# Attention scores in four quarters of TensorE, keys kept in halves of a tile, and a later landing in the planner's model

## The chip, the cores and the metric

One core of a Trainium2 chip runs the kernel. The metric is the device time of one execution in microseconds; of several runs the median counts. The trace that is read here comes from one profiled execution of the kernel before the change.

## What is computed

Three layers follow each other on 4 sequences of 576 tokens with 512 features (2304 tokens, 18 tiles of 128 tokens). The reference, cut to what matters:

```python
scores = scale * q @ k.T                     # 8 heads of 64, per sequence
mask = (rel >= 0) & (rel < 128)              # each query sees itself and 127 keys before it
attn = softmax(where(mask, scores - slope * |rel|, -1e9))
x = attn @ v                                 # attention
u = x + (relu(x.T @ w_tok1) @ w_tok2).T      # token mixing, 256 hidden
x = u + relu(u @ w_ch1) @ w_ch2              # first wide layer, 1536 hidden
out = x + relu(layernorm(x) * g @ w2_ch1) @ w2_ch2   # second wide layer, 2048 hidden
```

## The kernel before

**Attention.** A loop goes over the 18 tiles of 128 queries. `packed` issues the scores of one tile and the values of the tile two before it as one block on TensorE (PE). Heads are taken in two halves c of four heads. For each head pair p and each head j of the pair, one matmul contracts the 64 features on 64 rows of the array (row half j), against the keys of the tile before and of the own tile: 64 rows, 128 queries as columns, 256 keys streamed. The program has 8 such matmuls for a tile; the profile shows each fp32 matmul as two instructions. `softmax` then folds the two key tiles into one: a predicated copy (L631) on VectorE (DVE) puts the earlier key's score where the own key lies after the query, so that each query keeps 128 scores. Bias, minimum, Exp on ScalarE (ACT), four transposes on PE, a copy and two masks on GpSimd (POOL) follow. Keys lie in a ring of four tiles (`keys`); tile i uses slot i % 4, and where that is slot 0 the matmul reads slots 0 and 3.

**Token mixing** runs in between: tok1 and tok2 matmuls (L440 to L442, L735 to L737) of one sequence after the other. They need `wt1` (5 pieces) and `wt2` (4 pieces).

**Conversions.** All weights come as 64-bit floats. `load_f64` fetches two strided views of a piece (`rh`, one buffer; `rw`, two buffers), ACT makes `e` from `rh` (L416), and DVE makes the fp32 weight in four instructions (L419 to L431). The next load of `rh` waits until `e` has been made. Attention contains 21 conversions: 9 of `wt1` and `wt2`, then 12 of the first wide layer. Of these 12, six go straight into the six buffers `w`, and six are written to DRAM (`stage_w`) and fetched again later. The first wide layer's first eight tiles need 24 such pieces in six steps: two pieces of w_ch1 and two of w_ch2 for a step. Each step is a group of "products" (matmuls b, L993 to L995), and its "second" (matmuls acc, L1048 to L1050) runs one step later. The order in which the pieces are used: products 0, products 1, second 0, products 2, second 1, products 3, second 2, and so on, two pieces each.

**The planner.** The order of all instructions on every engine is made when the kernel is built. `Plan.order` simulates the operations with fixed costs and latencies; each engine takes the ready operation with the lowest rank. The chip then runs each engine's list strictly in that order; only data is waited for, the planned times are not. What a conversion looks like in that model:

```python
LAT = {"PE": 400, "DVE": 260, "ACT": 290, "POOL": 180, "DMA": 4000, "CTL": 0}
ready[j] = max(ready[j], free[e] + self.lat(e, ...))      # an operation that needs k's result
rh = buf("raw", [P, DM, 4], I16, "rh", 1)                 # one buffer
op({"DMA": max(P * n * 8 / 360, 500)}, emit, writes=[x])  # load of rh, of rw
op({"ACT": act(n)}, ..., [rh], [e])                       # act(n) = 170 + 0.9 n
```

So in the model the next load of `rh` starts no sooner than load cost + 4000 + act(n) + 290 ns after the one before it. A piece has n = 256 (`wt1`), 288 (`wt2`) or 512 columns.

Of the kernel before, what the change touches and what calls it, by code (L numbers as in the profile page):

```python
# [10 lines left out]
F32 = mybir.dt.float32  # L11
# [3 lines left out]
I32 = mybir.dt.int32  # L15
# [8 lines left out]
B, H, S, D = 4, 8, 576, 64  # L24
P = 128
DM = H * D
NT = B * S
NTILE = NT // P
# [4 lines left out]
RING = 4  # L33
# [9 lines left out]
X_SHIFT, STAGE_SHIFT = -20, -20  # L43

STAGE_RATES = {(0, 2): 2, (1, 0): 2}
WARM, WARM_NS = 10, 320
WT_SHIFT, WT_START, WT_STEP, SHIFT_AT, W_START, W_STEP = 0, 2, 1, 7, 12, 2
SIGN16, EXP16 = 0x80008000 - (1 << 32), 0x7F807F80
# [2 lines left out]
def batches_of(i):  # L51

    out, t, end = [], i * P, (i + 1) * P
    while t < end:
        b, s = divmod(t, S)
        n = min(end - t, S - s)
        out.append((b, t - i * P, n, s))
        t += n
    return out
# [43 lines left out]
class Plan:  # L103
# [11 lines left out]
    HOLD_ANY = False  # L115
    AHEAD = 2000
    SPARE = {"DVE": 1200, "ACT": 0}
    LAT = {"PE": 400, "DVE": 260, "ACT": 290, "POOL": 180, "DMA": 4000, "CTL": 0}

    def __init__(self):  # L120
        self.pools, self.ops, self.rings, self.ctl = {}, [], {}, {}
# [4 lines left out]
    def buf(self, pool, shape, dtype, tag, bufs=1):  # L126
        b = Buf(self, pool, shape, dtype, tag, bufs)
        ring = self.rings.setdefault((pool, tag), [])
        if len(ring) >= bufs:
            b.after = [ring[-bufs]]  # L130
        if ring:
            b.behind = ring[-1]
        ring.append(b)
        return b
# [176 lines left out]
def pe(n):  # L311
    return 2.6 + n / 2.4


def block_kernel(tc, qT, kT, v, wt1, wt2, wa1, wa2, wb1, wb2, g, bias, out):
    nc = tc.nc
    NF1, NF2 = FF1 // P, FF2 // P
    pl = Plan()
    buf = pl.buf

    def op(cost, emit, reads=(), writes=(), behind=()):
        return pl.op(cost, (lambda e: emit()) if len(cost) == 1 else emit, reads, writes, behind)
# [26 lines left out]
    after = buf("const", [P, P], F32, "after")  # L349
# [31 lines left out]
    def load_f64(src, k, n, dst=None, get=None):  # L381

        rh = buf("raw", [P, DM, 4], I16, "rh", 1)
        rw = buf("raw", [P, DM, 2], U32, "rw", 2)
        e = buf("cvt", [P, DM], BF16, "e", 1)
        s = buf("cvt", [P, DM], BF16, "s", 1)  # L390
        m = buf("cvt", [P, DM], U32, "m", 1)
        at = k * P * n * 8
        flat = src.bitcast(U8).rearrange("r b -> (r b)")

        def rows(x, first):
            return x.rearrange("p n t -> p (n t)"), flat[first:first + P * n * 8].rearrange("(p b) -> p b", p=P)

        def head(dt):
            return rh.t[:, :n, 3].bitcast(dt) if dt != I16 else rh.t[:, :n, 3]

        def load_half(x, first):
            def emit():
                out, in_ = rows(x.t[:, :n].bitcast(U8), first)
                nc.sync.dma_start(out=out, in_=in_)

            op({"DMA": max(P * n * 8 / 360, 500)}, emit, writes=[x])

        load_half(rh, at)
        load_half(rw, at + 3)

        def half(x):
            return x.t[:, :n].bitcast(I32)

        op({"ACT": act(n)}, lambda: nc.scalar.activation(  # L416
            out=e.t[:, :n], in_=head(BF16), func=AF.Copy, scale=2.0 ** -116), [rh], [e])

        op({"DVE": 1.3 * dve(n // 2, True)}, lambda: nc.vector.tensor_scalar(  # L419
            half(s), half(e), 3, EXP16, ALU.logical_shift_left, ALU.bitwise_and), [e], [s])  # L420
        op({"DVE": 1.3 * dve(n // 2)}, lambda: nc.vector.scalar_tensor_tensor(
            out=half(s), in0=half(e), scalar=SIGN16, in1=half(s), op0=ALU.bitwise_and, op1=ALU.bitwise_or), [e], [s])
        op({"DVE": 1.3 * dve(n, True)}, lambda: nc.vector.tensor_scalar(
            m.t[:, :n], rw.t[:, :n, 0], 4, None, ALU.logical_shift_left), [rw], [m])
        if dst is None:
            dst = y = buf("cvt", [P, DM], F32, "y", 2)

            def get():
                return y.t[:, :n]

        op({"DVE": 1.3 * dve(n)}, lambda: nc.vector.scalar_tensor_tensor(  # L431
            out=get(), in0=m.t[:, :n], scalar=2.0 ** 32, in1=s.t[:, :n], op0=ALU.add, op1=ALU.mult), [m, s], [dst])
        return dst, get
# [28 lines left out]
    src = {"a1": wa1, "a2": wa2, "b1": wb1, "b2": wb2}  # L462
    wtiles, staged = [], {}
    used = [0]

    def convert_w(x, dst=None, get=None):

# [53 lines left out]
        return [buf("hid", [P, 2, S + P], F32R, "few" + p) for p in "hl"]  # L521


    keys = buf("att", [P, RING, H // 2, P], F32, "keys")
    wt1h, wt1l = ([buf("tok", [P, 5, TOK], F32R, f"wt1{x}{odd}") for odd in range(2)] for x in "hl")
    wt2h, wt2l = few()
    vs, qs = {}, {}
# [1 line left out]
    def load_qk(i):  # L529
        r = i % RING  # L530
        b = qs[i] = buf("att", [P, H // 2, P], F32, "q", Q_BUFS)
        op({"DMA": 1000}, lambda: nc.sync.dma_start(out=keys.t[:, r].rearrange("p h t -> p (h t)"), in_=kT[i]),
           writes=[(keys, r)])
        load(b, lambda: b.t.rearrange("p h t -> p (h t)"), P * DM * 4, qT[i])

    def load_v(i):
# [25 lines left out]

    def keys_of(i):

        s = i % RING
        if starts_batch(i):
            return [i], 0, 0, (s, s + 1, 1)
        table = 3 if len(batches_of(i)) > 1 else 2 if len(batches_of(i - 1)) > 1 else 1
        if s == 0:
            return [i, i - 1], 0, table, (0, RING, RING - 1)  # L570
        return [i - 1, i], 1, table, (s - 1, s + 1, 1)

    pv = buf("psb", [P, H // 2, P], F32, "ps_v")
    rs_t, xh_t, xl_t = {}, {}, {}
# [1 line left out]
    ps_t, pf_t = {}, {}  # L576

    def packed(i, i2):

        parts, ready = [], []
        if i is not None:
            tiles, own, table, (a0, a1, a2) = keys_of(i)
            w = len(tiles) * P
            x = qs[i]
            for c in range(2):
                ps_t[i, c] = buf("psa", [P, 2, 2, 2 * P], F32, "ps_s", 2)  # L590

                def scores(c=c, ps=ps_t[i, c]):
                    for p in range(2):
                        for j in range(2):
                            r = slice(j * D, (j + 1) * D)
                            nc.tensor.matmul(ps.t[:, j, p, :w], x.t[r, 2 * c + p], keys.t[r, a0:a1:a2, 2 * c + p],  # L596
                                             start=True, stop=True)

                parts.append((4 * pe(2 * w), scores, [x] + [(keys, t % RING) for t in tiles], [ps_t[i, c]]))
        if i2 is not None:  # L600
            tiles2 = keys_of(i2)[0]
            na = len(tiles2)
            for c in range(2):
                def values(c=c, pf=pf_t[i2, c]):
                    for p in range(2):
                        for a, kt in enumerate((i2, i2 - 1)[:na]):
                            for j in range(2):
                                nc.tensor.matmul(pv.t[j * D:(j + 1) * D, 2 * c + p], vs[kt].t[:, 4 * c + 2 * p + j],  # L608
                                                 pf.t[:, a, 2 * p + j], start=(a == 0), stop=(a == na - 1))

                parts.append((na * 440, values, [(pf_t[i2, c], a) for a in range(na)] + [vs[kt] for kt in tiles2],
                              [(pv, c)]))

        before = None
        for k, (cost, emit, reads, writes) in enumerate(parts):
            also = parts[k + 1:] if k == 0 else []
            now = op({"PE": cost + (200 if k in (0, len(parts) - 1) else 0)}, emit,
               reads + [x for p in also for x in p[2]], writes + [x for p in also for x in p[3]])
            if before is not None:
                pl.chain[before] = now  # L620
            before = now

    def softmax(i, c):

        tiles, own, table, _ = keys_of(i)
        na = len(tiles)
        ps = ps_t[i, c]
        o = slice(own * P, (own + 1) * P)
        if na == 2:
            b = slice((1 - own) * P, (2 - own) * P)  # L630
            op({"DVE": 690}, lambda: nc.vector.copy_predicated(  # L631
                ps.t[:, :, :, o], after.t.bitcast(I32).unsqueeze(1).unsqueeze(1).to_broadcast([P, 2, 2, P]),
                ps.t[:, :, :, b]), [ps, after], [ps])
        t = buf("att", [P, 4, P], F32, "t", T_BUFS)
        mn = buf("small", [P, 4], F32, "mn", 3)
        for m in range(4):
            op({"DVE": 358}, lambda m=m: nc.vector.tensor_tensor_reduce(  # L637
                out=t.t[:, m], in0=ps.t[:, m % 2, m // 2, o], in1=bias_sb.t[:, table, 4 * c + m],
# [6 lines left out]
        for m in range(4):  # L645
            op({"ACT": 580}, lambda m=m: nc.scalar.activation(  # L646
                out=pr.t[:, m], in_=t.t[:, m], func=AF.Exp, bias=mn.t[:, m:m + 1], scale=-1.0,
# [433 lines left out]
    def swap(close=(), open_=()):  # L1081
# [6 lines left out]

        pl.control(emit, close, [n for n, _ in open_])

    rest = attention()

# [25 lines left out]
    for s in range(len(steps) + 1):  # L1120
# [5 lines left out]
        layer, c, tiles, n = steps[s]  # L1126
        hid = {}
        if len(tiles) == 2:
            parts, ns = two_blocks(w1, xs, hid), (4, 4)
        else:  # L1130
            parts, ns = seven_products(w1, xs, keep, s == len(steps) - 1, hid), (2, 3, 3, 0)
# [81 lines left out]
```

## Time and profile before

| | us |
|---|---|
| median of 3 runs | 855.08 (854.54 to 855.89) |
| profiled execution, its own time | 856.19 |
| its span in the trace | 854.5 |

The 1.7 us between the span and the execution's own time lie around the program. Engines are PE (matmul), PEld (weight load), DVE, ACT, POOL and SP (the queue that issues most DMAs). A matmul's end is modelled in the trace, so busy PE may hide small gaps; starts are measured.

### The profile page before, as it was taken

To read this page: it belongs to the slowest core of one execution; us is meant where nothing else is said; L and a number is where in the kernel's file an instruction comes from. 1 tells how busy PE (TensorE), PEld (TensorE's weight loads), DVE (VectorE), ACT (ScalarE), POOL (GpSimd) and SP (SyncE) were. 2 spreads that over 40 slices of the span, in tenths; PEclk is the share of its full clock that TensorE was granted. 3 is DMA by queue.
4 is the path that set the end of the run, shared out by engine and by line. 5 is a ranking of instruction groups with operands and counts; after the bars stand their busy time and mean duration, and the time that the engine had idled before them with its cause. 6 is when DMAs were issued, how large, how long until landed. Compare 5 with 4: busy or idle time off the path is not lost.

```text
span 854.5 us, 13205 instructions
## 1 busy us (share of the span) xinstructions
PE 830.8 (97%) x4478; PEld 685.8 (80%) x4478; DVE 638.1 (75%) x1311; ACT 394.3 (46%) x952; POOL 338.5 (40%) x353
## 2 busy tenths in 40 slices
PE   7999999979999999999999999999999999999997
PEld 6777888758888887788887888788889888888885
DVE  5787777987887989987888956988676855555554
ACT  6888766643434535334357323336357422222220
POOL 2685445554433556532235524614234612221110
PEclk9999999999999999999999999999999999999999
DMA  8678736457677699978762521887477762221112
GB/s 296 187 207 265 242 103 213 146 179 241 200 234 240 228 324 337 348 252 268 264 210 74 178 92 48 264 263 258 154 259 234 247 198 74 74 75 49 50 50 98
DMA packets 73698, 164.96 MB, mean 193 GB/s; under 512 B 8352, under 2 KB 8480, under 8 KB 73632
## 3 DMA queue, kind: packets, MB, share of 16 engines
q1 hardware_dynamic: 73152, 162.83, 57.5%
q0 software_dynamic: 480, 1.31, 0.7%
q8 instruction: 35, 0.57, 0.3%
q14 instruction: 31, 0.25, 0.1%
HBM read 131.34 MB, written 31.46 MB: 191 GB/s over the span
## 4 chain that ended last, share of the span: by engine, by line
PE 83%; DVE 7%; ACT 4%; DMA 2%; issue 2%; POOL 1%; SPq 1%; ACTq 0%; DVEq 0%; POOLq 0%
PE acc L1048 12%; PE acc L1050 12%; PE acc L1049 12%; PE b L993 9%; PE b L995 9%; PE b L994 9%; PE ps_v L608 3%; PE ps_s L596 3%; PE p L848 1%; PE b L442 1%; PE b L441 1%; PE b L440 1%; PE ps_t L653 1%; DVE st L374 1%; PE tok L735 1%
## 5 line engine op out<-in xcount | busy, mean ns | idle before, releaser
L1053 DVE TENSOR_TENSOR u<-acc,u 128x512 f32<-128x512 f32 x252 | 172.9, 687 | 64.0 <-PE acc L1050 60.6
L1048 PE MATMUL acc<-w2h,hh 128*128 128x512 f32 x504 | 198.6, 394 | 5.3 <-DVE u L1053 4.7
L1050 PE MATMUL acc<-w2h,hl 128*128 128x512 f32 x504 | 196.6, 390 | 0.3 <-DVE hl L926 0.2
L1049 PE MATMUL acc<-w2l,hh 128*128 128x512 f32 x504 | 196.5, 390 | 0.0
L924 ACT ACTIVATE hh<-b 128x512 fp32r<-128x512 f32 (+1 forms) x140 | 74.5, 552 | 262.8 <-PE b L995 226.4
L993 PE MATMUL b<-xh,w1h 128*128 128x512 f32 x392 | 154.0, 393 | 3.6 <-DVE hl L926 3.4
L994 PE MATMUL b<-xl,w1h 128*128 128x512 f32 x392 | 153.3, 391 | 1.8 <-DVE xl L374 1.8
L995 PE MATMUL b<-xh,w1l 128*128 128x512 f32 x392 | 153.4, 391 | 0.2 <-DVE w1l L374 0.2
L926 DVE SCALAR_TENSOR_TENSOR hl<-b,hh 128x512 fp32r<-128x512 f32 (+1 forms) x140 | 85.8, 631 | 62.9 <-ACT hh L924 62.1
L374 POOL TENSOR_TENSOR w1l<-w,w1h 128x512 fp32r<-128x512 f32 (+1 forms) x53 | 67.6, 1275 | 134.0 <-ACT w1h L361 124.2
L1048 PEld LDWEIGHTS acc<-w2h,hh 128*128 128x128 f32 x504 | 94.7, 188 | 27.0 <-DVE u L1053 7.5
L1050 PEld LDWEIGHTS acc<-w2h,hl 128*128 128x128 f32 x504 | 94.6, 188 | 21.2 <-DVE hl L926 1.2
L1049 PEld LDWEIGHTS acc<-w2l,hh 128*128 128x128 f32 x504 | 94.7, 188 | 18.4
L374 POOL TENSOR_TENSOR w1l<-st,w1h 128x512 fp32r<-128x512 f32 x38 | 51.1, 1346 | 116.5 <-ACT w1h L361 103.2
L993 PEld LDWEIGHTS b<-xh,w1h 128*128 128x128 f32 x392 | 73.9, 189 | 19.8 <-DVE hl L926 3.8
L994 PEld LDWEIGHTS b<-xl,w1h 128*128 128x128 f32 x392 | 74.0, 189 | 17.4 <-DVE xl L374 2.3
L995 PEld LDWEIGHTS b<-xh,w1l 128*128 128x128 f32 x392 | 73.9, 189 | 16.1 <-DVE w1l L374 0.6
L416 ACT ACTIVATE e<-rh 128x512 bf16<-128x512 bf16 (+2 forms) x65 | 41.3, 635 | 74.0 <-DMA rh<-wb 33.6
L646 ACT ACTIVATE pr<-t,mn 128x128 f32<-128x128 f32 x144 | 55.9, 392 | 15.1 <-DVE mn L637 14.9
L663 POOL TENSOR_SCALAR_AFFINE_SELECT pf<-pf 128x512 f32<-128x512 f32 x64 | 42.3, 661 | 37.7 <-ACT pf L361 35.5
L374 DVE TENSOR_TENSOR b<-b,p 128x512 f32<-128x512 f32 x56 | 39.0, 697 | 23.6 <-PE b L995 23.1
L374 POOL TENSOR_TENSOR w2l<-w,w2h 128x512 fp32r<-128x512 f32 x23 | 32.1, 1395 | 46.1 <-ACT w2h L361 46.0
(118 smaller groups left out, 1369.3 us busy)
## 6 DMA issues: line engine op xcount, KB each, us to landing
w<-d SPq DMA_DIRECT2D x88, 256.0 KB, 4.6
rw<-wb SPq DMA_DIRECT2D x32, 512.0 KB, 4.5
rh<-wb SPq DMA_DIRECT2D x32, 512.0 KB, 4.7
rw<-wa SPq DMA_DIRECT2D x24, 512.0 KB, 4.5
rh<-wa SPq DMA_DIRECT2D x24, 512.0 KB, 4.5
d<-y SPq DMA_DIRECT2D x32, 256.0 KB, 4.4
keys<-kT SPq DMA_DIRECT2D x18, 256.0 KB, 4.3
q<-qT SPq DMA_DIRECT2D x18, 256.0 KB, 4.7
```

Of the source, the lines that this page charges most:

```text
L374: pl.op({e: cost[e] for e in on}, lambda e: ENGINE[e].tensor_tensor(get(), ga(), gb(), alu), [*several(a), *several(b), *also], several(dst))
L646: op({"ACT": 580}, lambda m=m: nc.scalar.activation(out=pr.t[:, m], in_=t.t[:, m], func=AF.Exp, bias=mn.t[:, m:m + 1], scale=-1.0, accum_o ...
L663: op({"POOL": 630}, lambda a=a: nc.gpsimd.affine_select(pf.t[:, a], pf.t[:, 1], [[0, 4], [1 - 2 * a, P]], (ALU.is_ge, ALU.is_gt)[a], 0.0, ...
L924: op({"ACT": act(n, True)}, lambda: nc.scalar.activation(out=hh.t[:, c], in_=go(), func=AF.Relu), [o], [(hh, key)])
L926: mark[0] = op({"DVE": dve(n)}, lambda: nc.vector.scalar_tensor_tensor(out=hl.t[:, c], in0=go(), scalar=0.0, in1=hh.t[:, c].bitcast(F32), ...
L993: nc.tensor.matmul(g.t, wh.t[:, w], xh.t, start=start and k == 0, stop=False, skip_group_check=True)
L994: nc.tensor.matmul(g.t, wh.t[:, w], xl.t, start=False, stop=False, skip_group_check=True)
L995: nc.tensor.matmul(g.t, wl.t[:, w], xh.t, start=False, stop=stop and k == 1, skip_group_check=True)
L1048: nc.tensor.matmul(o.t, hh.t[:, c:c + P], wh.t, start=j == 0, stop=False)
L1049: nc.tensor.matmul(o.t, hh.t[:, c:c + P], wl.t, start=False, stop=False)
L1050: nc.tensor.matmul(o.t, hl.t[:, c:c + P], wh.t, start=False, stop=j == 1)
L1053: op({"DVE": dve(DM)}, lambda o=o, i=i: nc.vector.tensor_tensor(u[i].t, o.t, u[i].t, ALU.add), [o], [u[i]])
```

## The change

1. A tile with two key tiles gets 16 score matmuls instead of 8: queries are cut into halves q of 64 as well. Half q needs keys only from the 192 that begin at key 64 q, so each matmul is 64 rows by 64 columns with 192 keys streamed. Tiles that begin a sequence (2 of 18) keep the matmuls that they have, four for a half of the heads.
2. `keys` holds five tiles, each in two halves of 64 keys; the last of every four tiles is loaded into two slots, so that 192 neighbouring keys are always one stretch.
3. The predicated copy becomes two, each of half the columns; the second takes 64 partitions.
4. In the planner's model, an operation of an engine that does not exist ("LATE", 1 ns, latency 5000) stands between the load of `rh` or `rw` and its readers, for the 21 conversions within attention. It emits no instruction.

```diff
+LATE_NS = 5000
-    LAT = {"PE": 400, "DVE": 260, "ACT": 290, "POOL": 180, "DMA": 4000, "CTL": 0}
+    LAT = {"PE": 400, "DVE": 260, "ACT": 290, "POOL": 180, "DMA": 4000, "CTL": 0, "LATE": LATE_NS}
...
         load_half(rh, at)
         load_half(rw, at + 3)
+        if late[0]:
+            op({"LATE": 1}, lambda: None, [rh], [rh])
+            op({"LATE": 1}, lambda: None, [rw], [rw])
...
-    keys = buf("att", [P, RING, H // 2, P], F32, "keys")
+    keys = buf("att", [P, (RING + 1) * 2, H // 2, D], F32, "keys")
+    def span(r, h, first, n):
+        return keys.t[r, first // D:(first + n) // D, h]
...
-        op({"DMA": 1000}, lambda: nc.sync.dma_start(out=keys.t[:, r]..., in_=kT[i]), writes=[(keys, r)])
+        for j in (r + 1, 0) if r == RING - 1 else (r + 1,):
+            op({"DMA": 1000}, lambda j=j: nc.sync.dma_start(out=keys.t[:, 2 * j:2 * j + 2]..., in_=kT[i]),
+               writes=[(keys, j)])
...
-                    for p in range(2):
-                        for j in range(2):
-                            r = slice(j * D, (j + 1) * D)
-                            nc.tensor.matmul(ps.t[:, j, p, :w], x.t[r, 2 * c + p], keys.t[r, a0:a1:a2, 2 * c + p], ...)
+                        for q in range(2):
+                            for j in range(2):
+                                r, m = slice(j * D, (j + 1) * D), slice(q * D, (q + 1) * D)
+                                nc.tensor.matmul(ps.t[m, j, p, q * D:q * D + 3 * D], x.t[r, 2 * c + p, m],
+                                                 span(r, 2 * c + p, a0 * P + q * D, 3 * D), ...)
...
-            op({"DVE": 690}, lambda: nc.vector.copy_predicated(
-                ps.t[:, :, :, o], after.t..., ps.t[:, :, :, b]), [ps, after], [ps])
+            for rows, c0 in ((P, D), (D, 0)):
+                op({"DVE": 430}, lambda rows=rows, c0=c0: nc.vector.copy_predicated(
+                    ps.t[:rows, :, :, P + c0:P + c0 + D],
+                    after.t[:rows, c0:c0 + D]...,
+                    ps.t[:rows, :, :, c0:c0 + D]), [ps, after], [ps])
...
+    late[0] = True
     rest = attention()
+    late[0] = False
```

The planner's cost of a half of the scores of such a tile goes from 4 x 215.9 to 8 x 82.6 ns. The keys are laid out in halves on the host.

## Rows read from the trace of the kernel before

**Rows 1.** The page: span, and busy time of the engines.
```profile
span 854.5 us, 13205 instructions
PE 830.8 (97%) x4478; PEld 685.8 (80%) x4478; DVE 638.1 (75%) x1311; ACT 394.3 (46%) x952; POOL 338.5 (40%) x353
```
**Rows 2.** Windows: us, busy us of PE, PEld, DVE, ACT, POOL; clock, DMA share, GB/s.
```profile
40.00:60.00 20.00, 19.75 (x193) 15.60 (x192) 15.09 (x57) 17.55 (x65) 15.16 (x23) 1.00 0.66 192
120.00:140.00 20.00, 20.00 (x178) 16.45 (x177) 14.79 (x56) 13.72 (x45) 10.77 (x15) 1.00 0.50 149
160.00:180.00 20.00, 16.16 (x73) 12.39 (x73) 19.76 (x28) 11.60 (x22) 13.62 (x12) 1.00 0.43 131
```
**Rows 3.** Chain that ended last, within 116 to 130: start us, us, what.
```profile
118.25 1.93 PE ps_s L596 x16
120.17 1.90 PE ps_v L608 x32
```
**Rows 4.** Timeline of PE, 99.2 to 101.2: start us, us, instructions.
```profile
99.25 2.00 PE L596 MATMUL ps_s<-keys,q 64*128 64x256 f32 x16
101.17 0.33 PE L608 MATMUL ps_v<-pf,v 128*64 128x128 f32 x2
```
**Rows 5.** Groups by form, 0 to 330: count, busy us, mean ns, idle before.
```profile
L631 DVE COPY_PREDICATED ps_s<-after,ps_s 128x512 f32<-128x512 int32 x32 | 21.9, 693 | 9.0 <-PE ps_s L596 8.4 <-issue 0.4
...
L926 DVE SCALAR_TENSOR_TENSOR hl<-b,hh 128x256 fp32r<-128x256 f32 x12 | 4.9, 417 | 1.8 <-ACT hh L924 1.5
```
**Rows 6.** Tile ps_s: duration ns min/median/max, first and last start.
```profile
L631 DVE COPY_PREDICATED ps_s<-after,ps_s x32: 667/696/697, 8.6 to 128.8; 128x512 f32<-128x512 int32 x32
```
**Rows 7.** The page, DMA issues: KB each, median us from issue to landing.
```profile
w<-d SPq DMA_DIRECT2D x88, 256.0 KB, 4.6
...
keys<-kT SPq DMA_DIRECT2D x18, 256.0 KB, 4.3
```
**Rows 8.** Waits within 0 to 140: us in total, times, longest.
```profile
ACT e L416 <- DMA rh<-wt: 1.5, 2, 1.1
```
**Rows 9.** Windows of line 416 alone: us, ACT busy us (instructions), clock, DMA.
```profile
0.00:80.00 80.00, 4.00 (x9) 0.98 0.78 237
80.00:176.00 96.00, 8.05 (x12) 1.00 0.53 171
176.00:280.00 104.00, 7.99 (x12) 0.98 0.70 228
```
**Rows 10.** Timeline of ACT: first and 21st conversion, and later ones.
```profile
15.25 0.43 ACT L416 ACTIVATE e<-rh 128x256 bf16<-128x256 bf16 x1 [1.14 <-DMA rh<-wt]
...
174.25 0.65 ACT L416 ACTIVATE e<-rh 128x512 bf16<-128x512 bf16 x1
...
222.08 0.66 ACT L416 ACTIVATE e<-rh 128x512 bf16<-128x512 bf16 x1 [3.87 <-DMA rh<-wa]
...
240.56 0.67 ACT L416 ACTIVATE e<-rh 128x512 bf16<-128x512 bf16 x1 [3.25 <-DMA rh<-wa]
...
254.39 0.68 ACT L416 ACTIVATE e<-rh 128x512 bf16<-128x512 bf16 x1
```
**Rows 11.** Timeline of ACT and DVE: writing and splitting weights.
```profile
230.35 0.63 ACT L361 ACTIVATE w2h<-w 128x512 fp32r<-128x512 f32 x1 [1.51 <-DVE w L431]
...
245.44 0.69 DVE L431 SCALAR_TENSOR_TENSOR w<-m,s 128x512 f32<-128x512 uint32 x1
```
**Rows 12.** Timeline of PE: last tok, first b, second 4 and second 5.
```profile
170.96 0.40 PE L737 MATMUL tok<-hh,fewl 128*128 128x512 f32 x1
...
165.15 0.48 PE L993 MATMUL b<-xh,w1h 128*128 128x512 f32 x1
...
274.83 0.49 PE L1048 MATMUL acc<-w2h,hh 128*128 128x512 f32 x1
...
295.88 0.48 PE L1048 MATMUL acc<-w2h,hh 128*128 128x512 f32 x1
```

More of the change, by code (lines that the diff above doesn't have):

```diff
@@ L464, in block_kernel @@
     used = [0]
+    late = [False]
     def convert_w(x, dst=None, get=None):
@@ L531, in load_qk @@
         b = qs[i] = buf("att", [P, H // 2, P], F32, "q", Q_BUFS)
-        op({"DMA": 1000}, lambda: nc.sync.dma_start(out=keys.t[:, r].rearrange("p h t -> p (h t)"), in_=kT[i]),
-           writes=[(keys, r)])
+        for j in (r + 1, 0) if r == RING - 1 else (r + 1,):
+            op({"DMA": 1000}, lambda j=j: nc.sync.dma_start(out=keys.t[:, 2 * j:2 * j + 2].rearrange("p a h t -> p (a h t)"), in_=kT[i]),
+               writes=[(keys, j)])
         load(b, lambda: b.t.rearrange("p h t -> p (h t)"), P * DM * 4, qT[i])
@@ L563, in keys_of @@
     def keys_of(i):
-        s = i % RING
         if starts_batch(i):
[L567 to L571, printed above, removed]
+            return [i], 0
+        return [i - 1, i], 3 if len(batches_of(i)) > 1 else 2 if len(batches_of(i - 1)) > 1 else 1
     pv = buf("psb", [P, H // 2, P], F32, "ps_v")
@@ L585, in packed @@
         if i is not None:
-            tiles, own, table, (a0, a1, a2) = keys_of(i)
-            w = len(tiles) * P
+            tiles, table = keys_of(i)
+            a1 = i % RING + 2
+            a0, w = a1 - len(tiles), len(tiles) * P
             x = qs[i]
@@ L593, in scores @@
                     for p in range(2):
-                        for j in range(2):
-                            r = slice(j * D, (j + 1) * D)
-                            nc.tensor.matmul(ps.t[:, j, p, :w], x.t[r, 2 * c + p], keys.t[r, a0:a1:a2, 2 * c + p],
-                                             start=True, stop=True)
-                parts.append((4 * pe(2 * w), scores, [x] + [(keys, t % RING) for t in tiles], [ps_t[i, c]]))
+                        if len(tiles) == 1:
+                            for j in range(2):
+                                r = slice(j * D, (j + 1) * D)
+                                nc.tensor.matmul(ps.t[:, j, p, :w], x.t[r, 2 * c + p], span(r, 2 * c + p, a0 * P, w),
+                                                 start=True, stop=True)
+                            continue
+                        for q in range(2):
+                            for j in range(2):
+                                r, m = slice(j * D, (j + 1) * D), slice(q * D, (q + 1) * D)
+                                nc.tensor.matmul(ps.t[m, j, p, q * D:q * D + 3 * D], x.t[r, 2 * c + p, m],
+                                                 span(r, 2 * c + p, a0 * P + q * D, 3 * D), start=True, stop=True)
+                parts.append((4 * pe(3 * D if w > P else P) * (2 if w > P else 1), scores,
+                              [x] + [(keys, k) for k in range(a0, a1)], [ps_t[i, c]]))
         if i2 is not None:
@@ L623, in softmax @@
     def softmax(i, c):
-        tiles, own, table, _ = keys_of(i)
+        tiles, table = keys_of(i)
         na = len(tiles)
+        own = na - 1
         ps = ps_t[i, c]
@@ L629, in softmax @@
         if na == 2:
-            b = slice((1 - own) * P, (2 - own) * P)
-            op({"DVE": 690}, lambda: nc.vector.copy_predicated(
-                ps.t[:, :, :, o], after.t.bitcast(I32).unsqueeze(1).unsqueeze(1).to_broadcast([P, 2, 2, P]),
-                ps.t[:, :, :, b]), [ps, after], [ps])
+            for rows, c0 in ((P, D), (D, 0)):
+                op({"DVE": 430}, lambda rows=rows, c0=c0: nc.vector.copy_predicated(
+                    ps.t[:rows, :, :, P + c0:P + c0 + D],
+                    after.t[:rows, c0:c0 + D].bitcast(I32).unsqueeze(1).unsqueeze(1).to_broadcast([rows, 2, 2, D]),
+                    ps.t[:rows, :, :, c0:c0 + D]), [ps, after], [ps])
         t = buf("att", [P, 4, P], F32, "t", T_BUFS)
@@ L1186 @@
         arrays[f"{n}T"] = np.ascontiguousarray(a.transpose(3, 1, 2, 0, 4)).reshape(NTILE, P, DM)
+    arrays["kT"] = np.ascontiguousarray(arrays["kT"].reshape(NTILE, P, H // 2, 2, D).swapaxes(2, 3)).reshape(NTILE, P, DM)
     arrays["v"] = np.ascontiguousarray(x["v"].transpose(0, 2, 1, 3)).reshape(NT, DM)
```

## The prediction

> **What bounds the kernel now.** I read the page first: PE is busy for 97% of the span, DVE for 75%, ACT for 46% [rows 1]. PE's work is then the time wherever nothing starves it, and what matters is where the change shortens PE's work and where it may starve it. The windows say where to look. From 120 to 140 us, deep in attention, PE is busy throughout while DVE and ACT have 5 to 6 us of 20 to spare; early in attention, 40 to 60, ACT is nearly as full as PE; from 160 to 180, between the last token mixing and the first wide layer, DVE is the full one and PE idles [rows 2]. The chain agrees for attention: it runs through PE's own bursts, scores 1.93 us and values 1.90 us for a tile, back to back [rows 3]. So PE time taken from attention should shorten attention. The second view is that of the conversions, line 416, since the planner's new latency moves them. There are 21 by 176 us and 12 more by 280 [rows 9]; the first starts at 15.25, the 21st at 174.25 [rows 10], while the first product of the wide layer starts at 165.15 [rows 12]. The weights of that layer are thus made while attention runs, ahead of need, and the lead matters: from there on a conversion takes (254.39 - 222.08) / 5 = 6.46 us when they follow each other closely, with ACT waiting for the landing [rows 10], while a step of the wide layer, second 4 to second 5, takes 295.88 - 274.83 = 21.05 us [rows 12] and uses four of them, one per 5.26 us. Conversions are slower than their use; only the lead pays the difference.
>
> **The change, part by part.**
>
> *Scores.* The 16 score instructions of a tile run as pairs of the two row halves: 8 pairs of 256 columns take 1.93 us. The 32 value instructions run as 16 pairs of the two column halves, 128 columns each, and take 1.90 [rows 3]. Both move 2048 columns per pair of streams, and both take the same, so the time goes with columns (0.94 ns each), not with instructions. After the change there are 32 instructions of 192 columns. If four quarters run at once, they are 8 groups: 1536 columns, 1.45 us, 0.48 saved per tile. If only two run at once, 16 pairs: 3072 columns, 2.89 us, 0.96 lost. If the number of instructions binds, 32 take what the value burst's 32 take, 1.90, nothing gained. I take four at once, with some start-up left: row halves and column halves each already run side by side here, and quarters combine them. 0.41 us x 16 tiles = 6.5 us saved (bounds: 7.7 saved, 15.4 lost).
>
> The Trainium skill speaks against this: TensorE: Matmul & The Clock Gate, Part 1, says that without hardware decoding each matmul costs the sequencer some 62 ns, which binds once the array's work is shorter. By that rule 32 instructions take 1.98 us and the burst gains nothing. The trace tends the other way: 32 value instructions need 59 ns each [rows 3], and two of them start within the 30 ns from 101.17 to the edge of the window [rows 4].
>
> *Predicated copies.* 32 copies of 512 elements, 693 ns each, become 64 of 256. The nearest row of 256 elements from PSUM is 417 ns [rows 5], so a pair costs 834, 141 ns more: 4.5 us of DVE in all (bounds: 0 if cost went with size alone, 22 us if each half cost the whole). DVE's spare time in attention hides it [rows 2], and the scores end 0.2 us sooner per half of the heads, which covers the latency. The last copy starts at 128.8 [rows 6], well before DVE fills up after 160. Taken at 0; without that cover it would cost the 4.5.
>
> *Keys.* 18 loads of keys become 22 (tiles 3, 7, 11, 15 twice), 256 KB more each time on SP's queue, 4.3 us to land [rows 7], issued two tiles ahead of use. Behind them on SP wait a load of queries and the next load of `rh`, late by one issue. Taken at 0; if exposed, at most 4 x 4.3 = 17 us. The strided reading of keys (three runs of 64) is taken as free, as the two runs of a wrapped ring were.
>
> *The planner's latency.* It emits nothing, so its only effect is on the order. What could it win? ACT waits for a landing in attention twice, 1.5 us in all [rows 8]. That is the stall that it could remove; other reorderings may win or lose as much.
>
> What does it cost? `rh` has one buffer, so the model starts no load before the last one's `e`. By the code, the least distance of two conversions in the model is load + 4000 + act + 290 ns: 5.42 us for `wt1`, 5.54 for `wt2`, 6.38 for the wide layer. From the first to the 21st (4, 4 and 12 distances) that is 120.4 us, under the 159.0 that the trace shows; the model's landing time does not set the pace now. With 5000 more the distances are 10.42, 10.54 and 11.38, together 220.4. That is more than the 159.0: now it must set the pace, and the list puts the 21st conversion some 60 us further on in the work of the other engines, behind relus of the wide layer's first steps on ACT's queue. The chip need not wait as the model did, but ACT runs its list in order, and those relus wait for PE.
>
> So where does the 21st start on the chip? The lower end is today's place less the gain, 174.25 - 6.5 = 168; the upper is the model's, 15.25 + 5 + 220.4 = 241. I take 224, nearer the upper end, since the list ties the conversion to PE's steps, and 17 us short of it, since real landings let the conversions close up where the list does not hold them. An estimate; it is the uncertain number of this forecast.
>
> From there 12 more conversions must be made before second 5, and 10 before second 4, at 6.46 us each. From `e` to the split weight takes 245.44 + 0.69 - 240.56 = 5.57, and one 0.63 us instruction of ACT [rows 10, 11]: 6.2. With the 21st at 224, second 5 can start at 224 + 77.5 + 6.2 = 307.7. In the trace it starts at 295.88 [rows 12]. So 11.8 us are lost there, whatever attention gained. Pieces 7 to 12 also go to DRAM and back, 4.6 us for the fetch alone [rows 7], which makes second 1 and products 3 late as well; those stalls lie inside the same 11.8.
>
> Where this begins to bite: second 4 wants its weights at 274.83 - 6.5 = 268.3, so the 21st conversion must start by 268.3 - 64.6 - 6.2 = 197.5. Later than that, PE waits.
>
> **Sum.** 856.19 of the profiled execution + 11.8 = 868.0; the median of the runs is 1.1 lower: 866.9. I say 866. Nothing after second 5 is taken to change.
>
> **Rivals.**
>
> *The lead is enough (faster).* The chip closes the conversions up as soon as data allow, and the 21st starts before 197.5. For it: loads of other tiles land in 4.3 to 4.6 us [rows 7], not 9, and 23 us of lead are to spare (174.25 to 197.5). Against it: ACT's queue is in order, and the pace of 6.46 is already that of conversions following each other closely. Then the scores' gain stands: 855.1 - 6.5 = 848.6. The token mixing's own wt1 and wt2 also come later, which moves work on PE, not its sum.
>
> *Instructions bind, lead enough (same).* The scores gain nothing, no stall: 855.
>
> *Quarters do not run together (slower).* 16 x 0.96 = 15.4 us more in attention, PE being the bound there; the conversions use that time, so the two do not add: 855.1 + 15.4 = 870.5. For it: no row here shows four at once. Against it: each axis alone does.
>
> *The model's own pace holds on the chip.* The 21st at 241: 17 us on top of the forecast, 884. It is the end of my own case, not another one.
>
> **How the numbers follow.** The lead lost: 0.56. Lead enough with gain: 0.28. Instructions bind, no stall: 0.07. Quarters not together: 0.09. Two tenths of a per cent, 1.7 us, is about what a measurement of this kernel tells from no change. Slower 0.56 + 0.09 = 0.65, same 0.07, faster 0.28. The lost lead's own range, the 21st conversion from 212 to 241, is 855 to 884: second 5 from 295.7, today's place, to 324.7. The range for all reaches down to the faster rival, 846 with a little of the removed stall, and up to 884.
>
> **What would show it.** Score bursts of 1.45 to 1.55 us with 32 instructions; a burst of 1.9 or 2.9 shows a rival. Predicated copies near 420 ns. Line 416 by 176 us: about 15 to 17 times, not 21, and the 21st start near 224. Gaps on PE before acc (second 1, second 4), released by w2h or w2l and behind them DVE's w or the landing of `rh`; second 5 near 308. The forecast is wrong if the 21st starts before 198, or if PE shows no gaps between 200 and 310.

## The result and the profile after

The changed kernel took 860.13 us (median of 6 runs, 858.99 to 862.98), beside 854.01 for the kernel before on the same chip: a ratio of 1.0077, 95% interval [1.0062, 1.0093]. It is slower, inside the predicted range (846 to 884), by 6 us where the forecast had 11.8. Its profiled execution took 862.98, its span is 861.3, 6.8 more than before [rows 1].

The page: span and busy time.
```profile
span 861.3 us, 13752 instructions
PE 834.1 (97%) x4734; PEld 685.3 (80%) x4734; DVE 633.0 (73%) x1338; ACT 392.6 (46%) x952; POOL 344.1 (40%) x358
```
PE's share looks the same, so the shares say nothing of what happened. Windows of the changed kernel (us, busy us of PE, PEld, DVE, ACT, POOL; granted clock, DMA share, GB/s); the second, third and fourth stand beside [rows 2]:
```profile
0.00:20.00 20.00, 14.73 (x104) 10.60 (x108) 7.33 (x46) 10.25 (x40) 3.64 (x17) 0.73 0.92 317
40.00:60.00 20.00, 18.98 (x256) 14.59 (x249) 15.19 (x74) 17.39 (x66) 16.47 (x27) 1.00 0.82 217
120.00:140.00 20.00, 20.00 (x193) 16.36 (x187) 13.71 (x57) 12.01 (x41) 9.30 (x12) 1.00 0.30 107
160.00:180.00 20.00, 17.75 (x84) 13.48 (x83) 19.27 (x26) 13.33 (x25) 15.30 (x13) 1.00 0.28 93
180.00:200.00 20.00, 16.50 (x65) 13.10 (x64) 13.10 (x21) 5.53 (x10) 6.19 (x6) 0.83 0.54 178
```
The first and the last of these windows in the kernel before:
```profile
0.00:20.00 20.00, 15.16 (x112) 12.01 (x114) 10.44 (x60) 13.57 (x55) 5.04 (x19) 0.97 0.84 302
180.00:200.00 20.00, 17.91 (x78) 14.62 (x79) 13.51 (x24) 7.30 (x13) 5.11 (x6) 0.91 0.83 283
```
The quarters themselves do what the diff says. Timeline of PE at one tile:
```profile
119.25 1.53 PE L613 MATMUL ps_s<-keys,q 64*64 64x192 f32 x32
120.71 0.55 PE L626 MATMUL ps_v<-pf,v 128*64 128x128 f32 x6
```
32 score instructions, and the values follow 120.71 - 119.25 = 1.46 us after the first, where it was 1.92 [rows 3, 4]. Bursts that run through at the full clock take the same elsewhere in both kernels. The view by tile for ps_s (duration ns min/median/max, first and last start) gives the copies beside [rows 5, 6], and the place of the first and last quartered scores:
```profile
L613 PE MATMUL ps_s<-keys,q x512: 322/323/579, 11.5 to 129.9; 64*64 64x192 f32 x171
...
L651 DVE COPY_PREDICATED ps_s<-after,ps_s x64: 399/415/430, 13.2 to 132.7; 128x256 f32<-128x256 int32 x32, 64x256 f32<-64x256 int32 x32
```
So the saved PE time is there, 0.46 us x 16 tiles = 7.4 us (an estimate from these bursts), and yet the last token mixing and the first product of the wide layer come 1.65 and 1.05 us later than in [rows 12], and second 4 and second 5 come 9.85 and 6.98 us later. Timeline of PE of the changed kernel (last tok, first b, second 4, second 5):
```profile
172.61 0.40 PE L758 MATMUL tok<-hh,fewl 128*128 128x512 f32 x1
...
166.20 0.48 PE L1014 MATMUL b<-xh,w1h 128*128 128x512 f32 x1
...
284.68 0.39 PE L1069 MATMUL acc<-w2h,hh 128*128 128x512 f32 x1
...
302.86 0.48 PE L1069 MATMUL acc<-w2h,hh 128*128 128x512 f32 x1
```
By second 5 the whole loss of the span is there. It has two places, and both belong to the planner's longer landing.

**The start.** SP's queue now opens with loads of conversions, ahead of the first keys. Timeline of SP in the changed kernel, and its first line in the kernel before:
```profile
0.79 0.39 SPq L405 DMA_DIRECT2D rh<-wt  x1
1.24 0.89 SPq L405 DMA_DIRECT2D rw<-wt  x2
2.17 0.43 SPq L544 DMA_DIRECT2D keys<-kT  x1
```
```profile
0.79 0.39 SPq L532 DMA_DIRECT2D keys<-kT  x1
```
Its waits within 0 to 140 us (us in total, times, longest) show who pays:
```profile
DVE t L658 <- DMA bias_sb<-bias: 7.9, 1, 7.9
...
PEld ps_s L606 <- DMA keys<-kT: 2.1, 1, 2.1
...
PE ps_s L606 <- DMA q<-qT: 1.7, 1, 1.7
```
In the kernel before no wait of attention for keys, queries or the bias table is in that list; its one landing is [rows 8]. Behind these waits the granted clock of the first 20 us is 0.73, between the levels of 2.4 and 1.2 GHz, where the kernel before has 0.97. The bursts of the changed kernel show it: the scores of the second and third tile take 2.84 us, those of the fourth 1.53. Timeline of PE, the first four tiles of the changed kernel, then the first and the fourth of the kernel before:
```profile
7.67 1.16 PE L606 MATMUL ps_s<-keys,q 64*128 64x128 f32 x16 [1.74 <-DMA q<-qT]
...
11.54 2.84 PE L613 MATMUL ps_s<-keys,q 64*64 64x192 f32 x32
...
18.05 2.84 PE L613 MATMUL ps_s<-keys,q 64*64 64x192 f32 x32
...
25.90 1.53 PE L613 MATMUL ps_s<-keys,q 64*64 64x192 f32 x32
```
```profile
5.59 1.16 PE L596 MATMUL ps_s<-keys,q 64*128 64x128 f32 x16
...
19.17 3.53 PE L596 MATMUL ps_s<-keys,q 64*128 64x256 f32 x16
```
The first tile is 2.08 us late, the fourth 6.73; between the two lies the stretch at the lower clock. That the waits brought the clock down is likely, not shown: e13 below has a wait of PE for queries of 1.8 us at its start and keeps 1.00. At the first product of the wide layer the changed kernel is 1.05 late. In between, attention and mixing gained 5.7 us, beside the forecast's 6.5; some 1.5 of these (3.53 - 2.00, the burst of [rows 4]) only say that the kernel before runs its own fourth burst at the lower clock.

**The lead.** Line 416 is line 421 now. Windows of that line alone, beside [rows 9], and the 21st conversion, beside [rows 10]:
```profile
0.00:80.00 80.00, 3.98 (x9) 0.91 0.80 251
80.00:176.00 96.00, 6.01 (x9) 1.00 0.44 145
176.00:280.00 104.00, 8.59 (x13) 0.97 0.63 212
```
```profile
214.93 0.66 ACT L421 ACTIVATE e<-rh 128x512 bf16<-128x512 bf16 x1
```
18 conversions by 176 us instead of 21, and the 21st 40.7 us later than 174.25. By the forecast's own sum, second 4 can then start at 214.93 + 64.6 + 6.2 = 285.7; it started at 284.68.

PE did not stand idle for the 9.85 us by which second 4 is late. Windows of the changed kernel, in which PE's idle time from 220 to 300 is 2.7 us; in the kernel before PE is busy throughout those 80 us:
```profile
220.00:240.00 20.00, 19.51 (x86) 15.82 (x85) 17.53 (x30) 8.24 (x16) 8.71 (x7) 1.00 0.76 251
240.00:260.00 20.00, 19.22 (x86) 15.57 (x85) 16.29 (x28) 8.35 (x16) 8.74 (x8) 1.00 0.57 189
260.00:280.00 20.00, 19.39 (x90) 15.93 (x88) 17.35 (x30) 7.85 (x15) 6.89 (x7) 1.00 0.73 251
280.00:300.00 20.00, 19.22 (x86) 15.47 (x87) 19.29 (x31) 10.83 (x20) 12.40 (x9) 1.00 0.89 299
```
The list puts products of later steps ahead of second 4 instead: 240 b instructions start before it, where it was 222, and 36 instead of 54 between second 4 and second 5. So part of the lateness is work moved forward, and second 5, by which both kernels have started the same number of b and acc instructions, is the place to read the loss: 6.98.

**The clock.** Over the six runs of the changed kernel the mean granted clock of a run is 0.986 to 0.992, mean 0.989; over the 29 runs of the kernel before measured beside e5 below it is 0.993 to 0.998, mean 0.995. An estimate from these means: (1 - 0.989) x 860 = 9.5 us of full-speed time not granted, against (1 - 0.995) x 854 = 4.3. If PE had work in all of it, that is 5 of the 6 us. In the two profiled executions, (0.97 - 0.73) x 20 = 4.8 us of the difference lie in the first 20 us and (0.91 - 0.83) x 20 = 1.6 from 180 to 200.

### The profile page after: what moved, and what is told of

Same layout as the page of the kernel before. It is cut to its first block, busy times and chain, and to the rows that moved or that the text cites. A ratio compares the mean times of both kernels' runs of the same rounds, so it can differ in the third digit from the quotient of the medians.

```text
span 861.3 us, 13752 instructions
## 1 busy us (share of the span) xinstructions
PE 834.1 (97%) x4734; PEld 685.3 (80%) x4734; DVE 633.0 (73%) x1338; ACT 392.6 (46%) x952; POOL 344.1 (40%) x358
## 4 chain that ended last, share of the span: by engine, by line
PE 64%; DVE 4%; issue 2%; POOL 2%; ACT 1%; DMA 0%; POOLq 0%; DVEq 0%; ACTq 0%
PE acc L1069 11%; PE acc L1071 11%; PE acc L1070 11%; PE b L1014 8%; PE b L1016 8%; PE b L1015 8%; PE b L447 2%; PE b L446 2%; PE b L445 2%; PE p L869 1%; DVE st L375 1%; DVE u L1074 1%; POOL w2l L375 1%; DVE m L428 0%; POOL w1l L375 0%
## 5 line engine op out<-in xcount | busy, mean ns | idle before, releaser
L375 POOL TENSOR_TENSOR w2l<-w,w2h 128x512 fp32r<-128x512 f32 x24 | 34.4, 1436 | 45.8 <-ACT w2h L362 45.5
```

Source lines behind the costliest of these rows:

```text
L375: pl.op({e: cost[e] for e in on}, lambda e: ENGINE[e].tensor_tensor(get(), ga(), gb(), alu), [*several(a), *several(b), *also], several(dst))
```

## The experiments

Two parts of the change can be separated in the code, though each edit also changes the order as a whole; the first four kernels do that. Theory A: the longer landing costs the lead, the quarters gain. Theory B: the quarters do not pay. Theory C: only the late start costs.

**e1, without the longer landing.**
```diff
-    late[0] = True
+    late[0] = False
     rest = attention()
```


> The changed kernel without the planner's longer landing (quarters and keys in halves alone). Theory A, the lead of the conversions was lost: 21st conversion back near 174 us (167 to 176), first scores near 5.6 us, second 4 near 268 to 272, time 4 to 7 us under the kernel before (847 to 850). Theory B, the quarters themselves or their planning cost the time: as the changed kernel, 858 to 861. Theory C, only the late start of attention cost it: also 847 to 850, but then the next run tells A from C.

858.92 us, ratio 1.0055 [1.0031, 1.008]: slower than before, which neither A nor C allowed, and inside B's range (858 to 861): quarters with this order do not pay. First scores are at 5.1, the fourth tile's at 23.0 instead of 19.17; the 21st conversion, at 183.0, is well under what second 4, at 279.8, would have to wait for. So here the loss is in attention. Its waits within 0 to 140, and the timeline of ACT and PE around the longest:
```profile
ACT e L421 <- DMA rh<-wt: 7.7, 2, 3.9
```
```profile
18.25 0.43 ACT L421 ACTIVATE e<-rh 128x256 bf16<-128x256 bf16 x1 [3.92 <-DMA rh<-wt]
18.59 0.58 ACT L362 ACTIVATE ut<-ps_v 128x512 f32<-128x512 f32 x1
```
```profile
14.29 0.66 PE L674 MATMUL ps_t<-ident,pr 128*128 128x128 f32 x4
19.22 1.11 PE L696 MATMUL ps_v<-ident,ut 128*128 128x128 f32 x4 [4.27 <-ACT ut L362]
```
ACT stands 3.92 us at a conversion whose load has not landed; behind it on the list is the copy `ut` that PE needs; PE idles 4.27 us, and its next four transposes take 1.11 us instead of 0.66; the granted clock of the next window is 0.79. The same happens once more between 60 and 80 us:
```profile
20.00:40.00 20.00, 19.09 (x205) 14.75 (x204) 14.82 (x66) 15.18 (x59) 11.95 (x18) 0.79 0.54 168
60.00:80.00 20.00, 14.57 (x162) 10.57 (x150) 11.08 (x52) 14.28 (x51) 12.47 (x21) 0.91 0.96 250
```
The kernel before has 1.5 us of such waits [rows 8], this one 7.7. So there is a loss that the longer landing is there to remove, and the forecast had put it at 1.5.

**e2, the longer landing alone**, in the kernel before, for all 21.
```diff
         load_half(rw, at + 3)
+        if late[0]:
+            op({"LATE": 1}, lambda: None, [rh], [rh])
+            op({"LATE": 1}, lambda: None, [rw], [rw])
...
+    late[0] = True
     rest = attention()
+    late[0] = False
```

> The kernel before with nothing but the longer landing for the 21 conversions. Theory A (lead lost) and C (late start): 863 to 868, slower by about what the changed kernel lost (6.6) plus what the quarters save (about 6), 21st conversion near 215, first scores near 7.6 us. Theory B: within 2 us of the kernel before.

860.78 us, ratio 1.0069 [1.0044, 1.0094]: slower, with first scores at 8.2, the 21st conversion at 217.4, second 4 at 287.6. Both places of loss appear without the quarters, so the longer landing costs by itself; B falls as the whole cause. The size is 2 us under the expected.

**e3, ranks that do not count the longer landing.**
```diff
-                    late[d] = min(late[d], late[k] - self.lat(e, e2) - self.STRETCH * ops[d][0][e])
+                    late[d] = min(late[d], late[k] - (0 if e == "LATE" else self.lat(e, e2)) - self.STRETCH * ops[d][0][e])
```


> The changed kernel, but the ranks do not count the longer landing, so the loads of conversions get no earlier place on SP's queue at the start; the model still spaces the conversions. Theory A: first scores back near 5.6 us, but the 21st conversion later still (225 to 245), second 4 at 300 or later, 870 to 885. Theory C (the start is what cost): 854 to 857, faster than the changed kernel.

877.4 us, ratio 1.0273 [1.0245, 1.0301]. The first scores are back at 5.2 and the fourth tile's at 17.89, so it was the ranks that called the conversions' loads first. But the 21st conversion and second 4 (timeline of ACT, of PE) are later still:
```profile
231.97 0.65 ACT L421 ACTIVATE e<-rh 128x512 bf16<-128x512 bf16 x1
```
```profile
304.92 0.48 PE L1069 MATMUL acc<-w2h,hh 128*128 128x512 f32 x1
```
A holds, C as the only cause falls: the early call at the start was in part repaying the lead.

**e4, the longer landing for the 9 conversions of token mixing alone.**
```diff
-        if late[0]:
+        if late[0] and src is not wa1 and src is not wa2:
```


> The changed kernel with the longer landing for the 9 conversions of token mixing alone; the 12 of the wide layer are planned as before. Theory A: the lead is kept, 21st conversion 172 to 182, second 4 268 to 274, 847 to 853. If the delay of the token mixing's own weights costs: 855 to 860, with the first product of the wide layer later than 168.

849.92 us, ratio 0.9946 [0.9926, 0.9967]: faster than before. First scores at 5.9, 21st conversion at 172.9, second 4 at 269.3, no wait of ACT for a landing before 140. With the lead and the start kept and the landing waits gone, the quarters pay.

**e5, the longer landing for the 12 of the wide layer alone.**
```diff
-        if late[0]:
+        if late[0] and (src is wa1 or src is wa2):
```


> The changed kernel with the longer landing for the 12 conversions of the wide layer alone; the 9 of token mixing are planned as before. Through the one buffer of rh every conversion's rank depends on those behind it, so the first loads should still be called for early. Theory S (an early call for conversions costs the start): first scores at 7.5 to 8.5 us instead of 5.6, the fourth tile's scores after 23, 853 to 858. Theory L (only the lead costs): since the first nine come early, the 21st conversion lies at 172 to 185, second 4 near 269 to 273, 848 to 851.

853.47 us, ratio 0.9987 [0.9977, 0.9997]. SP again opens with rh, rw, rw; first scores at 7.2, fourth tile at 26.5. The lead is kept (21st at 182.0, second 4 at 272.3). So with the lead kept the early start costs some 3.5 us against e4, and the call comes from conversions at least nine places further back, through the one buffer `rh`. ACT also stands 7.2 us for landings here, which may be part of those 3.5; the run does not split the two. The mean granted clock of its runs is 0.985 to 0.994, in e4 0.995 to 0.998. The changed kernel, which opens its queue in the same way but loses the lead, took 6.7 us more than e5.

**e7, the setting of e4 in the kernel before** (e2, with e4's condition).
```diff
+        if late[0] and src is not wa1 and src is not wa2:
+            op({"LATE": 1}, lambda: None, [rh], [rh])
+            op({"LATE": 1}, lambda: None, [rw], [rw])
```

> The kernel before (whole scores, one copy, ring of four) with the longer landing for the 9 conversions of token mixing alone; beside the same planner setting with quarters, which took 849.9, it gives the worth of the quarters. Theory Q (the quarters give their 6 us once the order lets them): 854 to 857. Rival (the planner's setting alone is the gain, the quarters give nothing): 849 to 851.

854.68 us, ratio 1.0001 [0.9992, 1.001]. The setting alone gives nothing; with quarters it took 849.92, so the quarters are worth 4.8 us.

**e8, the longer landing for the two conversions at which e1 stood.**
```diff
+        count[0] += 1
-        if late[0]:
+        if late[0] and count[0] in (1, 8):
```


> The changed kernel with the longer landing for the 1st and the 8th conversion alone, the two on whose landing ACT stood 3.9 and 3.8 us when no conversion had it. Theory W (those two waits, with the slow clock behind them, are why quarters without a longer landing are slower): no wait of ACT for a landing over 1 us before 140, 849 to 853. Rival (the order as a whole): 855 to 859, the waits turn up at other conversions.

847.92 us, ratio 0.9928 [0.9907, 0.9949]: W holds, 1 us under its range and 11 under e1. No wait of ACT for a landing is left in its list before 140, and in the windows that showed e1's two stands the clock stays at full:
```profile
20.00:40.00 20.00, 19.44 (x267) 15.73 (x263) 16.94 (x88) 18.11 (x67) 14.45 (x22) 1.00 0.75 229
60.00:80.00 20.00, 16.66 (x221) 13.05 (x222) 16.94 (x76) 16.94 (x61) 12.12 (x19) 1.00 0.97 295
```

**e9, an accident of the order**, in the kernel before.
```diff
-    LAT = {"PE": 400, "DVE": 260, "ACT": 290, "POOL": 180, "DMA": 4000, "CTL": 0}
+    LAT = {"PE": 400, "DVE": 260, "ACT": 290, "POOL": 180, "DMA": 4050, "CTL": 0}
```

> The kernel before with the planner's landing time at 4050 ns instead of 4000, a change with no meaning of its own: how much does the order's accident weigh? If the order is robust: within 1.5 us of the kernel before. If accidents of the order are as large as what is studied here: 3 us or more away on either side.

856.62 us, ratio 1.0025 [1.0013, 1.0037]. A meaningless 50 ns move the time by 2 us, between the two expectations: a difference of that size between two orders need not come from the part that was edited. It is one such move; others may weigh more.

**e10, the setting of e8 in the kernel before** (e2, with e8's condition).
```diff
+        count[0] += 1
+        if late[0] and count[0] in (1, 8):
+            op({"LATE": 1}, lambda: None, [rh], [rh])
+            op({"LATE": 1}, lambda: None, [rw], [rw])
```

> The kernel before with the longer landing for the 1st and the 8th conversion alone; beside the same setting with quarters, which took 847.9, it gives the worth of quarters a second time. Theory Q (quarters worth 5 to 6 us): 852 to 855. Rival (the setting alone is the gain): 847 to 850.

856.33 us, ratio 1.0029 [1.0015, 1.0042]: the setting alone gives nothing here either; the time lies above both ranges. Beside e8 the quarters are worth 8.4 us; with e7 and e4, 4.8 to 8.4 around the 7.4 of the bursts, a spread of 3.6 where e9 moved 2.3.

**e11, a shorter lead without any longer landing in the wide layer**: e8 with the wide layer's conversions called for later.
```diff
-WT_SHIFT, WT_START, WT_STEP, SHIFT_AT, W_START, W_STEP = 0, 2, 1, 7, 12, 2
+WT_SHIFT, WT_START, WT_STEP, SHIFT_AT, W_START, W_STEP = 0, 2, 1, 7, 20, 2
```


> The changed kernel with the longer landing for the 1st and 8th conversion alone, and the wide layer's first conversion called for at the 20th half of a tile instead of the 12th (W_START), so that 8 instead of 12 lie in attention: the lead is shortened with no longer landing involved. Theory L: the start of the wide layer stays within 2 us (second 0 near 182), the 21st conversion comes at 190 to 210 instead of 168; where that is past 195, second 4 starts over 265.5 by 6.46 us for 6.46 us of lateness or so, time 850 to 862. Rival (the lead has slack of 40 us or more): second 4 at 264 to 267, time 846 to 850.

849.51 us, ratio 0.9948 [0.9928, 0.9969], 1.6 over e8. Its 21st conversion and second 4:
```profile
196.87 0.67 ACT L424 ACTIVATE e<-rh 128x512 bf16<-128x512 bf16 x1 [1.47 <-DMA rh<-wa]
```
```profile
268.27 0.39 PE L1072 MATMUL acc<-w2h,hh 128*128 128x512 f32 x1
```
29 us of lead less, and second 4 only 2.8 later than in e8: the first 26 us cost nothing, as the threshold of 195 had it. By its total, 849.5, the run lies in the rival's range (846 to 850), just under theory L's (850 to 862), and 1.6 is of e9's size, so the time does not tell the two apart. The place does: second 4 at 268.27 is above the rival's 264 to 267. The run passes the threshold by 2 us only; e2 and e3 pass it by more.

The forecast's sum for second 4, the 21st conversion + 70.8, over seven kernels (us, in the order of the 21st):

| run | 21st conversion | + 70.8 | second 4 measured |
|---|---|---|---|
| e8 | 168.2 | 239.0 | 265.5 |
| e4 | 172.9 | 243.7 | 269.3 |
| before | 174.25 | 245.1 | 274.83 |
| e11 | 196.87 | 267.7 | 268.27 |
| changed | 214.93 | 285.7 | 284.68 |
| e2 | 217.4 | 288.2 | 287.6 |
| e3 | 231.97 | 302.8 | 304.92 |

In the rows above e11 the sum lies 25 us or more under the measured start, so PE's own work sets second 4; from e11 on the sum gives it within 2.2 us. The other seven kernels belong to the upper rows: their 21st conversions start at 171.0 to 183.0, their second 4 at 263.6 to 279.8, 19 us or more above the sum.

**e12 and e13, two candidates for the best order**: 3500 ns for the 9 of token mixing, and 5000 for the first conversion alone.
```diff
-LATE_NS = 5000
+LATE_NS = 3500
...
-        if late[0]:
+        if late[0] and src is not wa1 and src is not wa2:
```


> The changed kernel with a longer landing of 3500 ns for the 9 conversions of token mixing alone, a candidate for the fastest order. If a smaller latency lifts the first loads less and still keeps ACT from standing: first scores near 5.5, no wait for a landing over 1 us, 845 to 849. Rival (too short for landings of 4.6 to 6.4 us behind the start's loads): a wait for a landing of 2 us or more comes back, 851 to 856.

848.02 us, ratio 0.9934 [0.9913, 0.9956]; first scores at 5.5, the longest wait of ACT for a landing 0.5 us.
```diff
-        if late[0] and count[0] in (1, 8):
+        if late[0] and count[0] in (1,):
```


> The changed kernel with the longer landing for the first conversion alone. Theory W (each of the two waits costs its length and the slow clock behind it): about half of the way from 858.9 to 847.9, 851 to 855, with a wait of ACT for a landing of 3 to 4 us left between 60 and 80. Rival (the first alone is the cause): 847 to 849.

845.55 us, ratio 0.9905 [0.9883, 0.9927], the fastest of all and under both kernels. W expected half of the way; the second wait is gone too. Its waits within 0 to 140 have
```profile
ACT e L424 <- DMA rh<-wt: 0.6, 1, 0.6
```
and nothing longer for `rh`. So the stand between 60 and 80 in e1 was no second cause; it went with the other order that follows from the first. W's half per wait falls; the rival (the first alone) holds, 1.5 us under its range. Why e13 lies 2.4 us under e8 was not followed up; it is of e9's size.

## Why the prediction was right or wrong

*Scores: right.* 1.45 forecast, 1.46 measured, four quarters at once; the sum used 0.41 a tile, and it was 0.46. The 32 instructions took 46 ns each. By the rule that was weighed against it (the Trainium skill, TensorE: Matmul & The Clock Gate, Part 1: without hardware decoding some 62 ns of sequencer for each matmul) they would have needed 1.98. The trace does not agree with that figure as a floor here; no run shows which way the instructions were decoded.

*Copies and keys: right.* 415 ns against 417. In the changed kernel no wait of PE in attention is put down to the copies beyond 0.2 us, or to keys beyond the 2.1 us at the start, which come from the order on SP.

*The planner's latency, spacing: right in kind, mis-sized, and in part lucky.* The single buffer of `rh` did set the pace, the 21st conversion moved past the threshold of 197.5, and the rule for second 4 held in four kernels. The term mis-sized is "I take 224": it was 214.9. One reason is visible: the first conversion starts at 9.51 rather than at 20, since its load now opens SP's queue. What else closed the conversions up was not measured. The gaps of PE that the forecast looked for between 200 and 310 are there, but small: 2.7 us. The rule for second 5 did not hold: with 214.93 it gives 214.93 + 77.5 + 6.2 = 298.6, a loss of 2.7 us, and second 5 came at 302.86, 6.98 later than before. The last conversion that it needs starts at 290.93, so its weights could be there by 297.1 (290.93 + 6.2, an estimate), and PE was still at work on what second 4 had held up. "So 11.8 us are lost there" is therefore 4.8 too large by two errors that go against each other, 9.1 us in the 21st conversion and 4.3 in what sets second 5.

*"Whatever attention gained": the gain was there but never reached the wide layer.* The forecast took the first products as 6.5 us earlier; they were 1.05 later, because attention's fourth tile was 6.7 us late: 2.1 by its first scores, the rest in a stretch at the lower clock, for which the forecast has no term. This is the step that failed: "it emits nothing, so its only effect is on the order" was followed for the spacing, not for the ranks, which the latency passes back from one conversion to the one before. e3 and e5 show it. The threshold stood all the same, since a late second 4 is set by weights and not by attention.

*"That is the stall that it could remove", 1.5 us: wrong.* It was read from the kernel before. With quarters the order changes and the same stand costs 7.7 us (e1), with idle PE and a slower clock behind it; orders without it are 11 to 13 us faster (e8, e13 beside e1), e9's 2 us of accident included.

*The rivals.* "The lead is enough" gave 848.6; the changed kernel is not that case, but e4, e8 and e12, which keep the lead, took 849.9, 847.9 and 848.0. "Instructions bind" and "quarters not together" fall with the bursts.

So the net 6 us are, along the runs: the quarters' gain (4.8 from e7 to e4), an early start that takes most of it back (3.5 from e4 to e5), and a lost lead (6.7 from e5 to the changed kernel), each to within e9's 2 us. The two losses share a cause, a latency put on 21 conversions where one was enough (e13).

## What to carry to other kernels

When a planner orders the instructions, a changed latency acts twice: on when it thinks data come, and through the ranks on what it calls for first; with a buffer of one, it acts on every operation of the chain. Cost a wait on an engine that runs its list in order by what stands behind it, and expect a shorter step elsewhere to bring such waits out. Before crediting an edit with 2 us, move a constant without meaning and see what the order's accident is worth.

## What the runs showed of the hardware

Four quarters of the array take fp32 matmuls side by side at no visible cost: 32 instructions of 64x64 weights and 192 columns in 1.46 us. The early stands cost more than their length: in e1, 4.27 us without work for PE were followed by a granted clock of 0.79 over 20 to 40 us, and a group of four transposes took 1.11 us instead of 0.66. In the changed kernel 32 score instructions took 2.84 us at 11.54, within the 20 us with a granted clock of 0.73, and 1.53 at 25.90. The mean granted clock of a run was 0.985 to 0.994 in the changed kernel, e1, e3 and e5, and 0.990 to 1.000 in all others.
